# Eight batches of windowed attention and a two-layer MoE block: the casts to bf16 issued head by head, and part of set-up's loads moved behind the last pair's weights

## The chip, the cores and the metric

The kernel runs on one core of a Trainium2 chip. The metric is the device time in microseconds, the median of several executions. The core's engines are called here by the profile's names: PE (TensorE), DVE (VectorE), ACT (ScalarE), POOL (GpSimd) and SP (the sync engine, which here only issues DMAs).

## The reference, cut to what matters

q, k and v are [8 batches, 8 heads, 576 tokens, 64], f32. Eight token indices are global.

```
scores = q k^T / sqrt(64)
mask = (|i - j| <= 32) or i is global or j is global
attn = softmax(scores where mask, else -1e9)
x = (attn v), heads side by side: [4608 tokens, 512]
h = x @ w_in                      # w_in [512, 2048]
g = h + sin(alpha * h)^2 / (alpha + 1e-9)
out = g @ w_out                   # w_out [2048, 512]
```

Everything comes in as f32; the kernel multiplies in bf16.

## The kernel before, in words

The batches are handled one after the other. For batch b there is attention over four pairs of heads (`attention`), then the first product with the snake function in 16 groups of 128 columns (`gemm1`, a group being eight matmuls of 288 columns on PE, sin and square on ACT or DVE, and the sum on DVE, L1150, into H2). The second product (`gemm2`) is a generator of single matmuls; `fill(n)` takes n of them. Those of batch b are strewn into the attention of batch b+1 and the products that follow, so that PE has work while ACT and DVE make the weights. The whole order is written out by hand: what stands in the Python text first stands first in its engine's queue, and each engine works through its own queue in order.

**Weights of attention.** For each pair hp, `scores` puts keys against queries in two halves g on PE, ACT takes the exponential into the tile E (L822), and DVE multiplies by the mask (`cover`, L831). `denominators` sums the weights, `numerators` multiplies by the values, and `normalise` writes the tile xT that `gemm1` reads (L908). In batch 0 the masks are applied after `beside(hp)`.

**Casts.** From batch 2 on, q, k and v of a batch are cast to bf16 by POOL's DMAs from DRAM to DRAM (qd, kd, vd). SP then loads them: `turn_q` and `turn_k` by DMA transpose, `load_v` plainly, `load_vg` for the global tokens' values. qd and vd are one DMA each (`cast_heads`, L334, 576 KB), kd is eight, one a head (`cast_k`, L339, 72 KB). `pace(src)` (L348) is a copy of one element by POOL into the tile `seen`: POOL waits in it until src is written, and all that it issues later waits with it. In `gemm1` of batches 1 to 5 one such copy, on the first group's result, stands ahead of all three casts of batch b+2, at the second group (`CASTS`). The casts of k and v of batch 2 stand in batch 0's `gemm1` at group 13, with no pace of their own.

**Set-up.** q and k of batches 0 and 1 are loaded "lying" (`load_lying`, L452) and turned on PE. v of batch 0 comes in twelve DMAs (`load_v0`, L387), with half of w_in (columns 0 to 1023) among them, in two loads of 512 KB (L422). SP meanwhile gathers the global rows of v. VGb, their cast on POOL (L594), waits for these gathers. Behind it POOL issues the lying loads of batch 1 with the second half of w_in (1024 KB), v of batch 1 (vd) and both halves of w_out (L428). alphaT is turned on PE at L671 and copied by ACT at L681; its reciprocal recipT is made on DVE in `set_recip`, called from `beside` after pair 1 of batch 0.

Of the kernel before, what the change touches and what calls it, by code (L numbers as in the profile page):

```python
# [16 lines left out]
P = 128  # L17
# [232 lines left out]
def kernel(  # L250
# [84 lines left out]

    def cast_k(b):
        cast[b, "kd"] = dramp.tile([KT, NT12, H, D], DT.bfloat16, name="kd")
        for h in range(H):
            nc.gpsimd.dma_start(  # L339
                out=cast[b, "kd"][:, :, h], in_=k[b, h].rearrange("(i a) d -> a i d", a=KT)  # L340
            )

# [41 lines left out]
    def load_v0():  # L384
        for half in range(2):
            for m in range(NT6):
                nc.gpsimd.dma_start(  # L387
                    out=VX[0][half * D : half * D + KT, m + half],
                    in_=v[0].rearrange("h (n m a) d -> n m a h d", n=2, a=KT)[half, m],
                )  # L390
            load_w_in((0,), slice(half * CT // 2, (half + 1) * CT // 2))

# [25 lines left out]

    def load_w_in(gs, cs=slice(0, CT)):
        for g in gs:  # L420
            cols = slice(g * DFF // 2, (g + 1) * DFF // 2)
            nc.gpsimd.dma_start(  # L422
                out=w_in[:, cs, cols], in_=moe_w_in[:, cols].rearrange("(c p) n -> p c n", p=P)[:, cs]
            )
# [167 lines left out]
    gather(v, gv)  # L592
    load_v0()
    nc.gpsimd.tensor_copy(out=VGb[:], in_=gv.rearrange("p h d -> p (h d)"))  # L594
    for hps in (early, late):
        for w in (1, 0):
            load_lying(1, w, hps)
        if hps == early:
            load_w_in((1,))
    gather_heads(k, gk)  # L600
# [69 lines left out]
    turn_lying(0, 0, banks_of[0])  # L670
    nc.tensor.transpose(out=both[:, 0:NT], in_=arow[:], identity=idf[0:NT, 0:NT])  # L671
    pg = [both[:, 32 + w * 32 : 64 + w * 32] for w in range(2)]
# [7 lines left out]
    place_lying(0, 1, 0, banks_of[0][1], act)  # L680
    act(out=alphaT[:], in_=both[:, 0:NT])  # L681
    place_lying(0, 0, 0, banks_of[0][0], dve)
# [27 lines left out]

    def set_recip():
        nc.vector.tensor_scalar(out=recipT[:], in0=alphaT[:], scalar1=1e-9, scalar2=None, op0=ALU.add)
        nc.vector.reciprocal(out=recipT[:], in_=recipT[:])
# [68 lines left out]
    def attention(b, beside):  # L782
# [136 lines left out]
        def first_batch():  # L919

            for hp in range(NHP):
                Es[hp] = pairp.tile([P, 2, NT6, WCOL], DT.bfloat16, name="E")
                for g in range(2):
                    scores(hp, g)
                    if hp == 0:
                        cover(hp, g)
                if hp == last:
                    for half in (1, 0):
                        edge_tile(half)
                    nc.gpsimd.tensor_copy(out=seen[0:1], in_=VX[0][0:1, NT6, 0, 0:1])  # L930
                    cast_v(1)
                    load_w_out((0, 1))
                beside(hp)
                for g in range(2 * (hp > 0)):
                    cover(hp, g)
                if hp:
                    denominators(hp - 1)
            release_ring()
            for hp in range(2):
                inverse(hp)  # L940
                first_numerators(hp)
            inverse(last - 1)
# [17 lines left out]
        for hp in range(NHP):  # L960
            Es[hp] = pairp.tile([P, 2, NT6, WCOL], DT.bfloat16, name="E")
            scores(hp, 0)
# [109 lines left out]
    TURNED, PLACED, GLOBALS = (4, 7, 10, 13), (5, 8, 11, 14), 12  # L1072
    CASTS, TURNS = 1, 1


    def gemm1(b):
# [23 lines left out]
        for nt in range(NT):  # L1100
# [5 lines left out]
            if b == 0 and nt == 1:  # L1106
# [152 lines left out]

    waiting, copied, at_group = [], [None], [None]  # L1260

# [15 lines left out]
    def phase_a(b_att, b_moe):  # L1277
        def beside(at):

            if b_att == 0:  # L1280
                copy = nc.vector.tensor_copy
                if at in (0, 2):
# [89 lines left out]
```

## Time and profile before

| | us |
|---|---|
| median of 3 runs | 343.97 |
| lowest and highest run | 343.32, 344.09 |
| the profiled execution, its time | 344.07 |
| the profiled execution, its span | 342.3 |
| PE busy in it | 314.9 |
| ACT, DVE, POOL busy | 278.5, 252.4, 94.4 |

The profile is one execution. A row of the timeline has the start and the length in us, the engine, the line, the operation, the tiles written and read, the shapes and the count; in brackets stand the engine's idle time just before and what ended it. "issue" there means that the engine waited for nothing that the profile shows. A DMA row has the size and the time from issue to landing. In the DMA view q0 is the queue of POOL's DMAs (software), q1 that of SP's (hardware) and q8 fetches instructions; the shares of a queue are of 16 engines' time, and overlapping packets can add up to more than 100%.

### The profile page before, as it was taken

How to read it: one execution, taken by the hardware profiler on the slowest of the kernel's cores; microseconds unless marked ns; L12 is line 12 of the kernel's file. 1: busy time of each engine (PE TensorE's matmuls, PEld its weight loads, DVE VectorE, ACT ScalarE, POOL GpSimd, SP SyncE). 2: the span in 40 equal slices, each digit the busy share in tenths (PEclk: the TensorE clock that was granted, in tenths of full speed). 3: DMA queues.
4: the chain of work that ended last, by engine and by line, in shares of the span. 5: the costliest groups of instructions: out<-in, count | busy, mean ns of one | idle time of the engine just before them, and what ended most of it. 6: DMA issues, size and time to landing. Idle time of an engine off the chain costs nothing.

```text
span 342.3 us, 11579 instructions
## 1 busy us (share of the span) xinstructions
PE 314.9 (92%) x4812; PEld 202.0 (59%) x4812; DVE 252.4 (74%) x484; ACT 278.5 (81%) x406; POOL 94.4 (28%) x132
## 2 busy tenths in 40 slices
PE   0758989899989999999999999999989999999994
PEld 0646764467546765566556765676556755665543
DVE  4856896677875888777876778678757888788930
ACT  6757988788989889988899889888888888889621
POOL 7955342325300830062203520073000000003600
PEclk9999999999999999999999999999999999999999
DMA  7999999989991999199937996199929111010232
GB/s 106 125 155 201 187 225 172 168 171 161 163 131 50 165 174 169 66 148 164 166 93 139 160 153 119 46 171 176 158 57 163 33 33 69 1 33 0 78 93 67
DMA packets 140195, 41.98 MB, mean 123 GB/s; under 512 B 125194, under 2 KB 134538, under 8 KB 140138
## 3 DMA queue, kind: packets, MB, share of 16 engines
q0 software_dynamic: 98352, 18.50, 68.6%
q1 hardware_dynamic: 41786, 22.69, 34.3%
q8 instruction: 38, 0.62, 0.8%
q14 instruction: 19, 0.16, 0.1%
HBM read 41.95 MB, written 20.77 MB: 183 GB/s over the span
## 4 chain that ended last, share of the span: by engine, by line
PE 73%; DMA 9%; SPq 5%; ACT 4%; issue 4%; DVE 3%; POOL 0%; DVEq 0%; ACTq 0%; POOLq 0%
PE zo L1202 34%; PE zn L1094 11%; PE zd L1094 9%; PE zr L1094 9%; DMA w_out<-in_moe_w_out_dram 8%; PE ring L814 3%; PE zd L862 2%; PE zn L862 2%; DVE H L1150 2%; SPq L514 2%; SPq L508 1%; ACT sb L1144 1%; ACT L980 1%; SPq L504 1%; DMA SQ<-in_q_dram 1%
## 5 line engine op out<-in xcount | busy, mean ns | idle before, releaser
L1202 PE MATMUL zo<-w_out,H 128*128 128x512 bf16 (+1 forms) x576 | 147.1, 377 | 0.9 <-DMA w_out<-in_moe_w_out_dram 0.6
L1094 PEld LDWEIGHTS <-w_in 128*128 128x128 bf16 x1024 | 99.6, 98 | 45.1 <-issue 9.9
L1202 PEld LDWEIGHTS <-H 128*128 128x128 bf16 x592 | 53.7, 98 | 46.7 <-issue 1.0
L1094 PE MATMUL zn<-xT,w_in 128*128 128x288 bf16 (+1 forms) x384 | 57.0, 287 | 3.2 <-DVE H L1150 3.2
L1094 PE MATMUL zr<-xT,w_in 128*128 128x288 bf16 x320 | 47.7, 287 | 0.3
L1150 DVE SCALAR_TENSOR_TENSOR H<-s,recipT,zn 128x576 bf16<-128x576 bf16 (+1 forms) x48 | 39.5, 822 | 11.4 <-ACT s L1147 7.0
L1094 PE MATMUL zd<-xT,w_in 128*128 128x288 bf16 x320 | 46.3, 288 | 0.3 <-DVE H L1150 0.2
L822 ACT ACTIVATE E<-ring 128x720 bf16<-128x720 f32 x46 | 35.8, 778 | 13.2 <-PE ring L814 12.5
L1144 ACT ACTIVATE sb<-zn,alphaT 128x576 bf16<-128x576 f32 (+1 forms) x48 | 35.6, 742 | 11.6 <-PE zn L1094 11.1
L339 POOL DMA_DIRECT2D kd<-in_k_dram x48 | 34.6, 1162 | 34.7 <-DMA qd<-in_q_dram 30.9
L1149 DVE TENSOR_TENSOR s<-sb 128x576 bf16<-128x576 bf16 (+1 forms) x70 | 32.6, 466 | 12.4 <-ACT sb L1144 12.2
L1147 ACT ACTIVATE s<-sb 128x576 bf16<-128x576 bf16 (+1 forms) x58 | 40.0, 689 | 1.8
L831 DVE TENSOR_TENSOR E<-E,MASKT 128x720 bf16<-128x720 bf16 x64 | 33.4, 528 | 9.8 <-ACT E L822 7.8
L1150 DVE SCALAR_TENSOR_TENSOR H<-s,recipT,zd 128x576 bf16<-128x576 bf16 (+1 forms) x40 | 32.9, 822 | 7.5 <-ACT s L1147 5.0
L1150 DVE SCALAR_TENSOR_TENSOR H<-s,recipT,zr 128x576 bf16<-128x576 bf16 (+1 forms) x40 | 32.9, 822 | 6.2 <-ACT s L1147 4.6
L1144 ACT ACTIVATE sb<-zd,alphaT 128x576 bf16<-128x576 f32 (+1 forms) x40 | 29.6, 739 | 5.2 <-PE zd L1094 5.1
L1144 ACT ACTIVATE sb<-zr,alphaT 128x576 bf16<-128x576 f32 (+1 forms) x40 | 29.6, 740 | 4.3 <-PE zr L1094 4.3
L1209 ACT COPY osb<-zo 128x512 f32<-128x512 f32 (+1 forms) x36 | 20.9, 580 | 10.9 <-PE zo L1202 7.2
L814 PEld LDWEIGHTS <-KX 64*64 64x64 bf16 x896 | 15.7, 112 | 21.6 <-issue 21.0
L1192 POOL COPY H<-H 128x11 bf16 (+1 forms) x16 | 7.2, 448 | 76.7 <-DVE H L1150 75.9
L348 POOL COPY seen<-H 1x1 bf16<-1x1 bf16 x5 | 0.9, 178 | 94.3 <-DVE H L1150 94.3
L779 ACT ACTIVATE R<-L,shift 128x576 f32<-128x576 f32 x32 | 24.8, 779 | 0.6 <-DVE xT L908 0.2
(165 smaller groups left out, 351.3 us busy)
## 6 DMA issues: line engine op xcount, KB each, us to landing
VF<-vd SPq DMA_DIRECT2D x14, 336.0 KB
vd<-in_v_dram POOLq DMA_DIRECT2D x7, 576.0 KB, 10.4
qd<-in_q_dram POOLq DMA_DIRECT2D x6, 576.0 KB, 12.6
kd<-in_k_dram POOLq DMA_DIRECT2D x48, 72.0 KB, 10.8
w_out<-in_moe_w_out_dram POOLq DMA_DIRECT2D x2, 1024.0 KB, 24.4
out_dram<-osb SPq DMA_DIRECT2D x7, 256.0 KB
out_dram<-osb SPq DMA_DIRECT2D x8, 224.0 KB
out_dram<-osb SPq DMA_DIRECT2D x8, 192.0 KB
```

Of the source, the lines that this page charges most:

```text
L339: nc.gpsimd.dma_start(out=cast[b, "kd"][:, :, h], in_=k[b, h].rearrange("(i a) d -> a i d", a=KT))
L779: nc.scalar.activation(out=R[:], in_=L[:], func=AF.Exp, scale=-1.0, bias=shift[:, 0:1])
L814: nc.tensor.matmul(out=z[half * D : (half + 1) * D, t, 0 : G3 * WCOL].rearrange("p (m x c) -> p m x c", x=2, c=60)[:, m % G3, :, c0:c1], l ...
L822: nc.scalar.activation(out=weights(hp, g), in_=z[:, :, 0 : G3 * WCOL], func=AF.Exp, scale=scale)
L831: nc.vector.tensor_tensor(out=Eg, in0=Eg, in1=MASKT[:, None, G3 * g : G3 * (g + 1), :].rearrange("p o m c -> p o (m c)").to_broadcast([P, ...
L1094: nc.tensor.matmul(out=h_part, lhsT=w_in[:, c, nt * P : (nt + 1) * P], rhs=xT[:, c, lo:hi], start=(c == 0), stop=(c == CT - 1), skip_group ...
L1144: nc.scalar.activation(out=sb[:, 0:W], in_=h, func=AF.Sin, scale=alphaT[:, nt : nt + 1])
L1147: nc.scalar.activation(out=s2[:, 0:W], in_=sb[:, 0:W], func=AF.Square)
L1149: nc.vector.tensor_tensor(out=s2[:, 0:W], in0=sb[:, 0:W], in1=sb[:, 0:W], op=ALU.mult)
L1150: nc.vector.scalar_tensor_tensor(out=H2[:, nt, r0 : r0 + W], in0=s2[:, 0:W], scalar=recipT[:, nt : nt + 1], in1=h, op0=ALU.mult, op1=ALU.add,)
L1202: nc.tensor.matmul(out=ops[:, cols], lhsT=H2[:, nt, blk * P : (blk + 1) * P], rhs=w_out[:, nt, cols], start=(nt == 0), stop=(nt == NT - 1) ...
L1209: nc.scalar.copy(out=osb[:, cols], in_=ops[:, cols])
```

## The change

There are three edits.

1. `cast_one` takes the place of `cast_k`, and from batch 2's v and k on each cast is one head (72 KB). In `gemm1` of batches 1 to 5, every group from the second on may begin with a pace copy on the group before and one or two heads: q and k of batch b+2, one head a group and the sixteenth with the fifteenth; in batch 1's `gemm1` two a group, v of batch 2 first. v of batch b+1 is cast during the attention of batch b (from b = 2): three heads beside pair 2, paced on the placed queries, three beside pair 3, paced on the pair's weights, two at the end, paced on pair 2's part of xT. k of batch 2 is cast beside the four pairs of batch 1's attention, two heads each, paced on the pair's weights. q of batch 2 stays one DMA where it was. In batch 1's `gemm1`, `load_v(2)` and `load_vg(2)` move from group 2 to group 7.
2. In set-up w_in is cut into a quarter behind v's loads, a quarter, and a half. The second quarter, the lying loads of batch 1 and the half are now issued in `first_batch`, beside pair 3, behind a pace copy on that pair's weights.
3. alphaT's turn, its copy (now on DVE) and recipT are made in `set_recip`, which is called behind the numerators of pair 1.

```diff
+    def cast_one(b, name, h):
+        src = {"qd": q, "kd": k, "vd": v}[name][b, h]
...
+            nc.gpsimd.dma_start(out=dst[:, :, h], in_=src.rearrange("(i a) d -> a i d", a=KT))
+        else:
+            nc.gpsimd.dma_start(out=dst[:, h], in_=src)
...
-            load_w_in((0,), slice(half * CT // 2, (half + 1) * CT // 2))
...
     load_v0()
+    load_w_in(0, 1)
     nc.gpsimd.tensor_copy(out=VGb[:], in_=gv.rearrange("p h d -> p (h d)"))
-    for hps in (early, late):
-        for w in (1, 0):
-            load_lying(1, w, hps)
-        if hps == early:
-            load_w_in((1,))
...
-    nc.tensor.transpose(out=both[:, 0:NT], in_=arow[:], identity=idf[0:NT, 0:NT])
...
-    act(out=alphaT[:], in_=both[:, 0:NT])
...
     def set_recip():
+        nc.tensor.transpose(out=zo[0][:, 0:NT], in_=arow[:], identity=idf[0:NT, 0:NT])
+        nc.vector.tensor_copy(out=alphaT[:], in_=zo[0][:, 0:NT])
...
                 if hp == last:
+                    pace(Es[hp][0:1, 0, 0, 0:1])
+                    load_w_in(1, 2)
+                    for hps in (early, late):
+                        for w in (1, 0):
+                            load_lying(1, w, hps)
+                        if hps == early:
+                            load_w_in(2, 4)
...
                 first_numerators(hp)
+            set_recip()
             inverse(last - 1)
...
-    CASTS, TURNS = 1, 1
+    TURNS, LATE = 1, 7
+    cast_at = {}
+    for bm in range(1, B - 2):
+        pieces = [(bm + 2, name, h) for name in ("qd", "kd") for h in range(H)]
+        pieces = [(2, "vd", h) for h in range(H)] * (bm == 1) + pieces
...
-            if 0 < b and b + 2 < B and nt == CASTS:
-                pace(H2[0:1, 0, r0 : r0 + 1])
-                cast_heads(b + 2, q, "qd")
-                cast_k(b + 2)
-                cast_v(b + 2)
+            if 0 < nt and cast_at.get((b, nt)):
+                pace(H2[0:1, nt - 1, r0 : r0 + 1])
+                for piece in cast_at[b, nt]:
+                    cast_one(*piece)
...
-            if 0 < b and b + 1 < B and nt == TURNS + 1:
+            if 0 < b and b + 1 < B and nt == (LATE if b == 1 else TURNS + 1):
...
-                cast_k(2)
-                cast_v(2)
...
-                if at == 1:
-                    set_recip()
...
+            if (b_att, at) in cast_beside:
+                if at == NHP:
+                    pace(xTs[b_att][0:1, 2, 0:1])
+                elif at == 2 and b_att > 1:
+                    pace(QX[(b_att + 1) % 2][0:1, 0, 1, PAD + 4 : PAD + 5])
+                else:
+                    pace(newest[0][0:1, 0, 0, 0:1])
+                for piece in cast_beside[b_att, at]:
+                    cast_one(*piece)
```

POOL's queue in set-up, before (VF0 is batch 0's v, H2 holds the lying loads, VGb the global values, vd the cast v of batch 1):

```order
L387 DMA VF_91<-in_v_dram 48x8x64 x6
L422 DMA w_in<-in_moe_w_in_dram 128x2x1024
L387 DMA VF_91<-in_v_dram 48x8x64 x6
L422 DMA w_in<-in_moe_w_in_dram 128x2x1024
L594 CAST VGb<-SQ 64x512
L452 DMA H_97<-in_k_dram 48x4x768
L452 DMA H_97<-in_q_dram 48x4x768
L422 DMA w_in<-in_moe_w_in_dram 128x4x1024
```

The same place now (E is the last pair's weights):

```order
L392 DMA VF_91<-in_v_dram 48x8x64 x12
L426 DMA w_in<-in_moe_w_in_dram 128x4x512
L599 CAST VGb<-SQ 64x512
L353 COPY seen<-E 1x1
L426 DMA w_in<-in_moe_w_in_dram 128x4x512
L456 DMA H_97<-in_k_dram 48x4x768
L456 DMA H_97<-in_q_dram 48x4x768
L426 DMA w_in<-in_moe_w_in_dram 128x4x1024
```

One of the two loads of 512 KB that stood ahead of VGb stands behind it now, and behind the new copy.

POOL's queue from the end of batch 0's products into batch 1's, before (KX and QX are batch 1's turned keys and queries, qd, kd and vd the casts; the first two casts are batch 2's, the last one batch 3's):

```order
L369 COPY KX_94<-kTg 128x4x12x8
L372 COPY QX_96<-qTg 128x4x7x4 x2
L339 DMA kd<-in_k_dram 576x1x64 x8
L334 DMA vd<-in_v_dram 4608x1x64
L348 COPY seen<-H_97 1x1
L334 DMA qd<-in_q_dram 4608x1x64
```

And in a later batch now, from the attention of batch 2 into its products (QX is batch 3's queries, E pair 3's weights, xT the attention's result, H the first group's result; vd is batch 3's, qd batch 4's):

```order
L353 COPY seen<-QX_96 1x1
L346 DMA vd<-in_v_dram 576x64 x3
L353 COPY seen<-E 1x1
L346 DMA vd<-in_v_dram 576x64 x3
L353 COPY seen<-xT 1x1
L346 DMA vd<-in_v_dram 576x64 x2
L353 COPY seen<-H_97 1x1
L346 DMA qd<-in_q_dram 576x64
```

Where POOL issued a whole cast behind one copy, it now issues one to three heads behind each.

More of the change, by code (lines that the diff above doesn't have):

```diff
@@ L334, in cast_heads @@
         nc.gpsimd.dma_start(out=cast[b, name][:], in_=src[b].rearrange("h s d -> s h d"))
[L336 to L341, printed above, removed]
+    def cast_one(b, name, h):
+        src = {"qd": q, "kd": k, "vd": v}[name][b, h]
+        tiles = name == "kd"
+        if h == 0:
+            cast[b, name] = dramp.tile([KT, NT12, H, D] if tiles else [S, H, D], DT.bfloat16, name=name)
+        dst = cast[b, name]
+        if tiles:
+            nc.gpsimd.dma_start(out=dst[:, :, h], in_=src.rearrange("(i a) d -> a i d", a=KT))
+        else:
+            nc.gpsimd.dma_start(out=dst[:, h], in_=src)
     def cast_v(b):
@@ L417, in values, with load_w_in @@
         return VX[b % 2][rows, i - half * (NT6 - 1), h, :]
-    def load_w_in(gs, cs=slice(0, CT)):
-        for g in gs:
-            cols = slice(g * DFF // 2, (g + 1) * DFF // 2)
+    def load_w_in(lo, hi):
+        if lo < hi:
+            cols = slice(lo * DFF // 4, hi * DFF // 4)
             nc.gpsimd.dma_start(
-                out=w_in[:, cs, cols], in_=moe_w_in[:, cols].rearrange("(c p) n -> p c n", p=P)[:, cs]
+                out=w_in[:, :, cols], in_=moe_w_in[:, cols].rearrange("(c p) n -> p c n", p=P)
             )
@@ L960, in attention @@
         for hp in range(NHP):
-            Es[hp] = pairp.tile([P, 2, NT6, WCOL], DT.bfloat16, name="E")
+            newest[0] = Es[hp] = pairp.tile([P, 2, NT6, WCOL], DT.bfloat16, name="E")
             scores(hp, 0)
@@ L1072 @@
     TURNED, PLACED, GLOBALS = (4, 7, 10, 13), (5, 8, 11, 14), 12
-    CASTS, TURNS = 1, 1
+    TURNS, LATE = 1, 7
[3 more added lines that the diff above has]
+        pieces = [(2, "vd", h) for h in range(H)] * (bm == 1) + pieces
+        each = 1 + (bm == 1)
+        for nt in range(1, NT):
+            cast_at[bm, nt] = pieces[(nt - 1) * each : nt * each if nt < NT - 1 else None]
+    cast_beside = {(1, hp): [(2, "kd", 2 * hp + h) for h in range(2)] for hp in range(NHP)}
+    for ba in range(2, B - 1):
+        for at, hs in ((2, range(3)), (3, range(3, 6)), (NHP, range(6, H))):
+            cast_beside[ba, at] = [(ba + 1, "vd", h) for h in hs]
     def gemm1(b):
@@ L1257, in gemm2_globals @@
         )
-    waiting, copied, at_group = [], [None], [None]
+    waiting, copied, at_group, newest = [], [None], [None], [None]
     def fill(n):
```

## The prediction

> **What bounds the kernel now.** I read the page first, then busy time by stage, then TensorE's idle gaps in the timeline, then GpSimd's timeline and the landings of its DMAs. The page's first rows show TensorE nearly full:
>
> ```profile
> PE 314.9 (92%) x4812; PEld 202.0 (59%) x4812; DVE 252.4 (74%) x484; ACT 278.5 (81%) x406; POOL 94.4 (28%) x132
> q8 instruction: 38, 0.62, 0.8%
> ```
>
> So only idle TensorE time can be won. The windows view, cut where the first group of products of each batch starts, shows where it is (columns: window, length, then busy time of PE, PEld, DVE, ACT, POOL, clock, DMA share, GB/s):
>
> ```profile
> 0.00:28.81 28.81, 14.68 (x569) 12.27 (x570) 18.00 (x63) 19.48 (x30) 22.81 (x45) 1.00 1.09 136
> 28.81:69.46 40.65, 36.48 (x740) 23.70 (x739) 30.74 (x54) 33.39 (x51) 13.81 (x17) 1.00 1.66 191
> 69.46:106.89 37.43, 35.83 (x529) 22.66 (x528) 28.75 (x53) 33.10 (x50) 9.94 (x11) 1.00 1.32 141
> ...
> 180.41:216.70 36.29, 36.29 (x535) 23.17 (x533) 28.18 (x52) 32.46 (x49) 9.92 (x11) 1.00 1.24 135
> 216.70:254.86 38.16, 36.71 (x535) 23.23 (x533) 28.18 (x52) 32.94 (x50) 9.92 (x11) 1.00 1.26 133
> 254.86:291.06 36.20, 36.20 (x533) 23.11 (x533) 29.07 (x51) 30.96 (x46) 0.00 (x0) 1.00 0.34 73
> ```
>
> The clock is full throughout. The window without casts (254.86 on: GpSimd 0.00, DMA share 0.34) takes 36.20 us with no TensorE idle time. The five with casts (69.46 to 254.86, 185.40 us) are 185.40 - 5 x 36.20 = 4.40 us longer together, but not alike: 1.23 the first, 0.09 the fourth, 1.96 the last. The gaps themselves, from TensorE's timeline (start, length, in brackets the idle time before and what ended it):
>
> ```profile
> 21.28 0.23 PE L814 MATMUL ring<-QX,KX 64*64 64x32 bf16 x1 [2.41 <-issue]
> 22.68 0.58 PE L708 MATMUL zo<-VGb,pick 64*128 64x512 bf16 x1 [0.85 <-POOL VGb L594]
> 56.20 2.10 PE L1202 MATMUL zo<-w_out,H 128*128 128x512 bf16 x9 [0.60 <-DMA w_out<-in_moe_w_out_dram]
> 68.02 0.21 PE L862 MATMUL zn<-E,VF 56*64 56x32 bf16 x4 [1.24 <-issue]
> 99.64 0.41 PE L862 MATMUL zd<-E,ones 56*64 56x120 bf16 x20 [0.87 <-issue]
> 249.10 0.49 PE L862 MATMUL zn<-E,VF 56*64 56x88 bf16 x27 [0.94 <-issue]
> ```
>
> The "issue" gaps fall in the middle of a run of like matmuls (the first alone follows as the last one of its fourteen, x1), all in stages of many short matmuls, and no semaphore ends them. TensorE lacked instructions. Those come by DMA: q8 above, 38 packets of 16 KB, and one of them lies just ahead of the gap at 99.64, while the software queue is full with the cast of v:
>
> ```profile
> q0 software_dynamic: 1695, 0.22, 127.9%
> q8 instruction: 1, 0.02, 2.3%
> ```
>
> That is the DMA view of 97.0 to 99.7 us. So I read the gaps as instruction fetches that share DMA engines with the casts. Against it stands the window from 180.41: casts like the others' and no gap.
>
> **The change part by part: set-up.** GpSimd's rows and the landing times (last number of a DMA row, from issue):
>
> ```profile
> 12.78 0.77 POOL L422 DMA_DIRECT2D w_in<-in_moe_w_in_dram  x1
> 17.22 0.79 POOL L422 DMA_DIRECT2D w_in<-in_moe_w_in_dram  x1
> 22.03 0.60 POOL L594 CAST VGb<-SQ 64x512 bf16<-64x512 f32 x1 [4.02 <-DMA SQ<-in_k_dram]
> 23.19 0.58 POOL L452 DMA_DIRECT2D H<-in_q_dram  x1
> 23.76 0.77 POOL L422 DMA_DIRECT2D w_in<-in_moe_w_in_dram  x1
> w_in<-in_moe_w_in_dram POOLq DMA_DIRECT2D x1, 1024.0 KB, 12.0
> H<-in_q_dram POOLq DMA_DIRECT2D x1, 288.0 KB, 6.8
> 21.55 0.77 ACT L822 ACTIVATE E<-ring 128x720 bf16<-128x720 f32 x1 [2.69 <-PE ring L814]
> 24.02 0.98 DVE L831 TENSOR_TENSOR E<-E,MASKT 128x720 bf16<-128x720 bf16 x2
> 14.61 0.21 DVE L712 TENSOR_SCALAR recipT<-alphaT 128x16 f32<-128x16 f32 x1
> 14.86 0.25 DVE L713 RECIPROCAL recipT<-recipT 128x16 f32<-128x16 f32 x1
> 28.43 27.72 DMA w_out<-in_moe_w_out_dram
> ```
>
> Before, two loads of 512 KB of w_in leave at 12.78 and 17.22. After, one leaves behind all twelve loads of v, at about 17.22 - 0.77 = 16.5; the second 512 KB waits for VGb's cast and the last pair's weights (call that moment T). The gathers that VGb waits for then share the DMA engines with 512 KB less. GpSimd has been idle for 4.02 us when VGb starts at 22.03, so it can come at 18.0 at the earliest, and no later than now unless the new load hinders the last gather. I take 19.5 to 20. With the 2.41 us gap halved, the weights (21.55 + 0.77) come about 1.2 earlier, so T is about 21 or a little before. TensorE then reaches the products up to 3.26 us earlier (2.41 + 0.85), at least 0; I take 1.8.
>
> What gives it back is w_out: its second half lands at 28.43 + 27.72 = 56.15, and TensorE was waiting already (0.60). The software queue's loads land in the order of issue: the last 1024 KB of w_in land at 23.76 + 12.0 = 35.8 and the load ahead of it at 23.19 + 6.8 = 30.0, so 512 KB cost 2.9 us. That much is moved behind T. But the queue was not full there (22 to 24, 24 to 26 and 26 to 28 us):
>
> ```profile
> q0 software_dynamic: 147, 0.27, 73.5%
> q0 software_dynamic: 100, 0.15, 75.9%
> q0 software_dynamic: 270, 0.39, 107.3%
> ```
>
> It lacked 0.12 + 0.24 MB of the 0.39 per 2 us, 1.8 us of transfer. So w_out lands 2.9 - 1.8 = 1.1 us later if T stays at 22.6, and about 0.6 us earlier if T comes 1.7 earlier. Whatever else TensorE wins in set-up it waits for here. Ends for set-up: -2.2 to +2.9; I take -0.6, the end nearer to the row with the wait. The loads that the products need have room: w_in's second half landed at 35.8 and its use begins eight groups of 1.2 us (below) after 28.81, at 38.4; the first 512 KB are wanted at 28.81.
>
> The pace copy on the last pair's weights stands before DVE's masking of the same tile (24.02 above), so DVE waits for GpSimd; at T of 21 to 22.8 that is hidden, and costs T - 24 if VGb slips past 24. Alpha's transpose, copy and the reciprocal move behind the numerators of pair 1: three DVE instructions of about 0.21, 0.21 and 0.25 us (the copy taken like L712) that stood off the path at 14.6 stand just before its sums of pair 2. DVE waits for ScalarE at places there, so I take +0.15, ends 0 and 0.67.
>
> **Batch 1's attention (28.81:69.46).** kd and vd of batch 2 no longer start behind w_out in one lump; kd goes two heads per pair, vd into the next products. The gap of 1.24 lay under that lump. I take -1.0, ends -1.24 and 0. turn_q(2) needs qd, which still follows w_out; its queries are placed at the very end of that attention, so 1 us late is covered.
>
> **Batches 2 to 6.** Per batch, one pace copy and three large groups of DMAs become 24 heads with 17 or 18 pace copies:
>
> ```profile
> 74.15 0.18 POOL L348 COPY seen<-H 1x1 bf16<-1x1 bf16 x1 [11.29 <-DVE H L1150]
> 74.82 2.20 POOL L334 DMA_DIRECT2D qd<-in_q_dram  x1 [0.49 <-issue]
> 87.72 0.64 POOL L339 DMA_DIRECT2D kd<-in_k_dram  x1 [6.00 <-DMA qd<-in_q_dram]
> kd<-in_k_dram POOLq DMA_DIRECT2D x48, 72.0 KB, 10.8
> qd<-in_q_dram POOLq DMA_DIRECT2D x6, 576.0 KB, 12.6
> 75.43 0.98 PE zr L1094 x8
> 76.63 0.98 PE zd L1094 x8
> ```
>
> GpSimd: 24 x 0.64 + 18 x 0.18 = 18.6 us against 9.9, of a 36 us period: hidden, as only casts queue behind its waits; its other late work, the columns' loads and copies of the last batch, comes after. The last two rows (chain of waits) put groups of products 1.20 us apart. One head per group takes 0.82 us, so pacing holds; with batch 1's two per group (1.46 us) GpSimd falls behind and those casts run as a stream until 74.2 + 12 x 1.46 = 91.7. Heads don't cost more transfer: kd went head by head before and landed in 10.8, whole qd in 12.6. On the sync queue the order is unchanged; load_v now waits for the last two heads of v, issued after pair 2's result, while pair 3 is still to be multiplied; it stands in the third group and its values are used a whole product stage later. Zero, at worst 0.5. The gain is the stalls: 0.87 + 0.94 seen, 4.40 at most by the periods. I take -1.6, ends 0 and -4.4: in attention six heads of v now fall in its second half, so not all go.
>
> Sum: -0.6 + 0.15 - 1.0 - 1.6 = -3.05 us on the profiled execution's 344.07 (span 342.3 and 1.8 around it; the median of the runs is 343.97, 0.1 less): 341.0.
>
> **The rivals.** *Stalls indifferent to the casts* (0.19): the window from 180.41 has casts and no gap. Then each gap returns at another place and only set-up and DVE count: 344.07 - 0.6 + 0.15, about 343.6, or 343.4 to 344.4. Here the Trainium skill speaks against the change ("DMA: Bandwidth & Descriptors", Queues, rings and completion order): each DMA engine goes round its queues packet by packet, so a fetch waits for a packet of each, however long the casts' backlog is; by that rule this rival is the case. The gap at 99.64 under a full queue speaks against it, the one at 249.10 for it: there the software queue was at 41.9%:
>
> ```profile
> q0 software_dynamic: 660, 0.08, 41.9%
> ```
>
> (246.0 to 249.1 us.) *w_out late* (0.13, slower): VGb does not come earlier, T stays at 22.6 or later, and the moved 512 KB delay w_out by 1.1 (queue as idle as before) to 2.9 us, straight into the wait at 56.20. With batches 2 to 6 unchanged this is 345.2 to 347.0, say 346.0. It decides from T of about 21.5 on: 22.6 less 1.1. *All idle goes* (0.08): 4.40, 1.24 and 0.6: 344.07 - 6.24 + 0.15 = 338.0.
>
> **How the numbers follow.** The forecast has 0.60, its own range 339.2 to 343.2 (half to one and a half times its gain). The range of 338.6 to 344.9 holds it, the indifferent stalls and the shallow end of the late w_out; outside stay most of the slower rival and of the largest gain, under 0.2. A measurement here tells 0.2%, 0.69 us, from no change. Faster by more: 0.60 + 0.08 + 0.06 of the indifferent case = 0.74; within: 0.12; slower: 0.14.
>
> **What would show it.** Right: the gap at 21.28 under 1.3 us, VGb's cast before 21, w_out's wait under 1 us, no issue gap over 0.5 us in batches 1 to 6 and periods of 36.2 to 36.6; GpSimd's waits for qd (6.00 above) gone. Wrong: TensorE waiting over 1.5 us for w_out, w_in or the lying loads; DVE waiting for GpSimd's pace copy; TensorE gaps of the same sum in other batches; the sync queue held at load_v so that stores are late.

## The result and the profile after

The changed kernel took 340.3 us (median of 8 runs, 339.32 to 341.94), the kernel before, run beside it, 344.03 (8 runs, 342.86 to 346.06). The ratio is 0.9891, with an interval of 0.9864 to 0.9919: faster, as forecast (341.0), by 0.7 us more. The profiled execution took 340.73 with a span of 339.0.

The windows of the changed kernel, cut where each batch's first product starts (columns as before):

```profile
0.00:28.41 28.41, 15.81 (x569) 12.57 (x570) 20.03 (x64) 20.51 (x29) 24.18 (x46) 1.00 1.09 137
28.41:68.15 39.74, 37.14 (x734) 24.12 (x738) 29.95 (x54) 32.42 (x50) 11.79 (x18) 1.00 1.50 188
68.15:104.69 36.54, 34.84 (x522) 22.71 (x529) 28.63 (x53) 33.04 (x50) 20.89 (x44) 1.00 1.41 144
104.69:141.63 36.94, 35.54 (x526) 23.17 (x533) 28.98 (x56) 32.90 (x50) 19.06 (x44) 1.00 1.19 134
141.63:177.89 36.26, 35.31 (x526) 23.19 (x533) 28.49 (x55) 32.20 (x49) 19.15 (x42) 1.00 1.32 139
177.89:214.30 36.41, 35.56 (x526) 23.22 (x533) 28.30 (x52) 32.53 (x49) 17.47 (x39) 1.00 1.27 136
214.30:251.73 37.43, 35.79 (x527) 23.23 (x534) 28.20 (x52) 32.89 (x50) 20.36 (x47) 1.00 1.38 135
251.73:287.90 36.17, 35.22 (x526) 23.09 (x533) 29.09 (x51) 31.00 (x46) 1.39 (x3) 1.00 0.49 84
```

Read the lengths only: this trace lacks records of some matmuls (x526 for PE where PEld has x533), so PE's busy time can't be set against before's. Set-up is 28.81 - 28.41 = 0.40 us shorter, the window of batch 1's attention 40.65 - 39.74 = 0.91, and the five with casts take 251.73 - 68.15 = 183.58 in place of 185.40, so 1.82 less. That makes 3.1 of the 3.3 us by which the span shrank. The last window before, 36.20, is 36.17 now. Each of these is one execution. How far one can be trusted is seen from the kernels below with the same set-up: their first products start between 28.04 and 28.95, so the 0.40 of set-up is not clear of that spread. Six more kernels with the casts as changed take 182.90 to 183.39 for the five windows, all well under 185.40.

TensorE's timeline at the places shown for before, and at the first products of batch 0:

```profile
19.08 0.51 PE L814 MATMUL zn<-QX,KX 64*64 64x120 bf16 x14 [0.51 <-issue]
19.52 0.61 PE L706 MATMUL zo<-VGb,pick 64*128 64x512 bf16 x1
23.93 0.51 PE L862 MATMUL zd<-E,ones 56*64 56x120 bf16 x16 [0.74 <-issue]
26.59 0.79 PE L862 MATMUL zd<-E,VF 56*64 56x88 bf16 x28 [0.75 <-DVE GD L756]
28.41 1.64 PE L1113 MATMUL zn<-xT,w_in 128*128 128x288 bf16 x6
29.85 1.64 PE L1113 MATMUL zr<-xT,w_in 128*128 128x288 bf16 x6
245.98 0.49 PE L862 MATMUL zn<-E,VF 56*64 56x88 bf16 x26 [0.24 <-issue]
```

From batch 1's attention on only one issue gap over 0.2 us is left, 0.24; w_out's wait and the gaps of 1.24, 0.87 and 0.94 are gone. In set-up the gap of 2.41 is 0.51 and the values' product (L706) comes 22.68 - 19.52 = 3.16 us earlier. Most of this is lost again before the products: a new issue gap (0.74), a new wait for DVE (0.75), and matmuls at half pace. Six products of 288 columns take 1.64 us, where before they took 0.90; the clock column says 1.00 all the same. GpSimd's timeline and, last row, DVE's:

```profile
18.09 0.80 POOL L599 CAST VGb<-SQ 64x512 bf16<-64x512 f32 x1 [0.77 <-DMA SQ<-in_k_dram]
19.47 0.18 POOL L353 COPY seen<-E 1x1 bf16<-1x1 bf16 x1 [0.58 <-ACT E L822]
19.70 0.76 POOL L426 DMA_DIRECT2D w_in<-in_moe_w_in_dram  x1
23.60 2.16 POOL L334 DMA_DIRECT2D vd<-in_v_dram  x1
24.05 2.12 DVE L712 TENSOR_SCALAR recipT<-alphaT 128x16 f32<-128x16 f32 x1
```

VGb's cast is there 3.9 us earlier and T is 19.5. The last row is the surprise: the 128x16 addition of the reciprocal, 0.21 us before, takes 2.12 where it now stands, and TensorE waits behind it (the 0.75 above). The median landing times on the page:

```profile
kd<-in_k_dram POOLq DMA_DIRECT2D x48, 72.0 KB, 4.6
vd<-in_v_dram POOLq DMA_DIRECT2D x48, 72.0 KB, 3.8
qd<-in_q_dram POOLq DMA_DIRECT2D x40, 72.0 KB, 6.3
```

k landed in 10.8 before and whole q in 12.6: a head no longer waits behind a batch's whole casts.

### The profile page after: what moved, and what is told of

It reads as the page before. It is cut to its first block, busy times and chain, and to the rows that moved or that the text cites. A ratio compares the mean times of both kernels' runs of the same rounds, so it can differ in the third digit from the quotient of the medians.

```text
span 339.0 us, 11821 instructions
## 1 busy us (share of the span) xinstructions
PE 310.8 (92%) x4753; PEld 202.9 (60%) x4812; DVE 253.9 (75%) x485; ACT 278.5 (82%) x405; POOL 142.5 (42%) x296
## 4 chain that ended last, share of the span: by engine, by line
PE 77%; DVE 7%; ACT 6%; issue 4%; DMA 3%; POOL 2%; DVEq 0%; POOLq 0%; ACTq 0%
PE zo L1218 32%; PE zn L1113 13%; PE zr L1113 10%; PE zd L1113 9%; PE ring L814 4%; DVE H L1166 3%; PE zd L862 3%; ACT sb L1160 2%; PE zn L862 2%; DVE s L1165 1%; DMA H<-in_q_dram 1%; DMA out_dram<-osb 1%; ACT L988 1%; ACT s L1163 1%; ACT L L772 1%
## 5 line engine op out<-in xcount | busy, mean ns | idle before, releaser
L1218 PE MATMUL zo<-w_out,H 128*128 128x512 bf16 (+1 forms) x517 | 134.3, 377 | 6.1 <-issue 5.1
L1113 PE MATMUL zn<-xT,w_in 128*128 128x288 bf16 (+1 forms) x384 | 58.0, 291 | 3.5 <-DVE H L1166 2.8
L1113 PE MATMUL zr<-xT,w_in 128*128 128x288 bf16 x320 | 48.5, 291 | 0.3
L344 POOL DMA_DIRECT2D kd<-in_k_dram x48 | 31.2, 653 | 9.1 <-issue 7.3
L346 POOL DMA_DIRECT2D vd<-in_v_dram x48 | 30.4, 643 | 1.8 <-issue 1.3
L346 POOL DMA_DIRECT2D qd<-in_q_dram x40 | 25.3, 633 | 8.2 <-issue 5.1
```

The costliest lines, as they stand in the source:

```text
L344: nc.gpsimd.dma_start(out=dst[:, :, h], in_=src.rearrange("(i a) d -> a i d", a=KT))
L346: nc.gpsimd.dma_start(out=dst[:, h], in_=src)
L1113: nc.tensor.matmul(out=h_part, lhsT=w_in[:, c, nt * P : (nt + 1) * P], rhs=xT[:, c, lo:hi], start=(c == 0), stop=(c == CT - 1), skip_group ...
L1218: nc.tensor.matmul(out=ops[:, cols], lhsT=H2[:, nt, blk * P : (blk + 1) * P], rhs=w_out[:, nt, cols], start=(nt == 0), stop=(nt == NT - 1) ...
```

## The experiments

**Theory.** TensorE's instructions come in blocks by DMA; a block whose fetch falls into a dense stretch of casts comes late, and TensorE stands. Spreading the casts takes them off the fetches. **Rivals**: the gaps belong to places in the program; smaller DMAs help, not their spreading; the gain is set-up's.

### Which edit gives what

*Casts alone, set-up alone, and everything but the moved reciprocal.* In the second k and v of batch 2 are cast where they were before; in the third alpha's turn and copy are back too:

```diff
 # casts only: edits 2 and 3 undone
+    for hps in (early, late):            # behind VGb's cast, as before
+        for w in (1, 0):
+            load_lying(1, w, hps)
...
 # set-up only: edit 1 undone
+            if 0 < b and b + 2 < B and nt == 1:
+                pace(H2[0:1, 0, r0 : r0 + 1])
+                cast_heads(b + 2, q, "qd")
+                cast_k(b + 2)
+                cast_v(b + 2)
...
 # all but edit 3
-            set_recip()                  # behind pair 1's numerators
...
+                if at == 1:
+                    set_recip()
```

> The kernel before with edit 1 alone: casts head by head, set-up and recipT as before. Forecast's theory (lumps of casts delay TensorE's instruction fetches, and w_out's load is not touched by them): the issue gaps of 1.24, 0.87 and 0.94 us go, set-up keeps its 2.41, 0.85 and 0.60; the sum of the windows of batches 2 to 6 falls from 185.4 to about 183.6; 341 to 342. Rival (fetch gaps are indifferent to casts, the gain is all set-up's): 343.5 to 344.3 and gaps of the same sum.

> The kernel before with edits 2 and 3 alone: whole casts as before. Forecast's theory: no gain in batches 2 to 6 (185 us for the five windows), set-up as in the changed kernel (VGb's cast near 18, the second quarter of w_in near 19.7), and the start of batch 1's products within 1 us of before's 69.46; 343 to 344.5. Rival (the gain is set-up's): 340 to 341.5.

> The changed kernel with edit 3 undone: alphaT turned and copied in set-up and recipT made beside pair 1, as before the change. In the changed kernel's profile the instruction that makes recipT took 2.12 us on DVE instead of 0.21, TensorE then waited 0.75 us, and its matmuls ran at 0.24 us apart instead of 0.12 until 31.9. Theory A (the late recipT stands behind GpSimd's issue of a whole cast, and the pause costs TensorE its clock): the wait and the slow matmuls go, products of batch 0 start at about 26 to 27 instead of 28.41 and the third group at about 31 instead of 34.20; w_out's landing takes back part; 338 to 339.5, against 340.3. Rival B (the slow matmuls come from the earlier start alone, or w_out takes all back): 340 to 341.

Measured: casts alone 341.6 us, ratio to before 0.9897 (0.9863 to 0.9931); set-up alone 343.49, 0.9955 (0.9926 to 0.9984); all but edit 3 340.54, 0.9871 (0.9832 to 0.991); the whole change, as above, 0.9891. So the casts bring nearly all of it. The two parts come to 1.03% and 0.45%, the whole to 1.09%; the intervals are too wide to say whether they add up. With casts alone no issue gap stands in batches 1 to 6 and the five windows take 183.33; with set-up alone they take 184.94 and gaps are back at the old places, the one of batch 2 only as 0.29 at 99.47 (TensorE's timeline of the set-up-only kernel):

```profile
68.42 0.21 PE L869 MATMUL zn<-E,VF 56*64 56x32 bf16 x3 [1.23 <-issue]
249.04 0.49 PE L869 MATMUL zn<-E,VF 56*64 56x88 bf16 x26 [1.30 <-issue]
```

Without edit 3 the addition takes 0.17 us, batch 1's attention starts at 52.05 in place of 53.45, and then w_out takes all of it back (TensorE's timeline of that kernel):

```profile
50.44 0.82 PE L1217 MATMUL zo<-w_out,H 128*128 128x512 bf16 x3 [0.52 <-DMA w_out<-in_moe_w_out_dram]
57.22 1.02 PE L1217 MATMUL zo<-w_out,H 128*128 128x512 bf16 x4 [1.83 <-DMA w_out<-in_moe_w_out_dram]
```

Its first product of batch 1 comes at 68.56, that of the whole change at 68.15, and its time is rival B's. In these kernels what set-up wins ends at w_out, and w_out itself does not come at a fixed time: its second half landed at 57.18 here, at 55.73 in the changed kernel and at 56.16 before. Theory A was right that the wait of 0.75 and the slow matmuls go, but batch 0's products start at 27.97, not at 26 to 27.

### Is it the fetches?

*Casts that nobody reads, put into the window without casts.* First early, at the second group of batch 6's products, then so late that they meet the fetches of batch 7's attention:

```diff
+            if b == B - 2 and nt == 1:        # the second kernel: nt == 13
+                pace(H2[0:1, nt - 1, r0 : r0 + 1])
+                cast_heads(B - 1, q, "qx")
+                for h in range(H):
+                    cast[B - 1, "kx", h] = dramp.tile([S, D], DT.bfloat16, name="kx")
+                    nc.gpsimd.dma_start(out=cast[B - 1, "kx", h][:], in_=k[B - 1, h])
+                cast_heads(B - 1, v, "vx")
```

> The changed kernel with one more lump, for nothing: in batch 6's products, the stage without casts, whole casts of q, k and v of batch 7 into scratch tensors, paced on the first group as the kernel before paced them. The output is unchanged. Forecast's theory (a lump delays fetches): gaps marked issue appear in batch 7's attention, the window from the start of batch 6's products to that of batch 7's grows from 36.17 by 0.5 to 2 us, the time by as much. Rival (indifferent): 36.2 to 36.4 and the time as the changed kernel's, 340.3.

> The changed kernel with one more thing: in the products of batch 6 at group 13, behind a pace copy on group 12 (about 268 us), whole casts of q, k and v of batch 7 to DRAM that nobody reads. In the changed kernel the stretch from the first product of batch 6 to that of batch 7 (251.7 to 287.9) has no casts, takes 36.17 us and has no TensorE gap; two or three instruction fetches fall between 268 and 290. Fetch theory (a fetch is slowed by packets of casts that are under way, and a late fetch stops TensorE): the fetches that start between about 270 and 288 come late against the instructions, an issue gap of 0.3 to 1.5 us appears in the attention of batch 7, and that stretch takes 36.5 to 37.7. Rival (the gaps were set by the program's places, and casts only happened to be there): no gap, 36.1 to 36.3. What comes after 287.9 may be longer for another reason, since the last batch's row loads queue behind the added casts; that part is not read.

The early lump changed nothing: window 36.17, no gap, 340.84 us (ratio 0.9892, 0.984 to 0.9944). My expectation missed that it had drained by about 275, before the next fetch. The late one hit: 342.49 us (0.9955, 0.9929 to 0.998). Its window, TensorE's timeline, and the DMA view from 276 to 278, just ahead of the fetch:

```profile
250.46:288.64 38.18, 36.37 (x533) 23.21 (x533) 29.33 (x51) 31.11 (x46) 9.93 (x14) 1.00 1.07 127
281.59 0.20 PE L862 MATMUL zd<-E,ones 56*64 56x32 bf16 x1 [1.81 <-issue]
q0 software_dynamic: 2219, 0.34, 236.6%
```

A window that takes 36.17 without casts takes 38.18, more than the 36.5 to 37.7 that I had expected, and an issue gap stands in a place that never had one. So the gaps come with the casts and aren't set by the program alone.

The DMA records give the start of each 16 KB instruction packet, and the records of TensorE's instructions how far it is by then. Packets are numbered from 0. A block is taken as 256 instructions of TensorE: a matmul and its weight load count two, and each of the 26 or 27 others on record (mostly waits on semaphores) counts one. The count in the table is what TensorE has begun when packet n starts, less 256 n. It can pass 256, since packet n need not bring block n.

```
kernel                      packet  start    count  TensorE stands
before                         8     65.46    396    66.78-68.02
before                        11     97.15    398    98.77-99.64
before                        28    246.66    412   248.16-249.10
changed                     8/11/28    -   301/306/323    -
no casts from batch 3 (below) 11/28    -     179/226      -
set-up only                   28    246.61    415   247.73-249.04
casts nobody reads, late      32    279.19    385   279.78-281.59
changed                       32    276.95    259      -
heads in a row (below)        15    137.49    447   138.24-140.07
whole but spread (below)      11     98.08    449    97.15-100.61
```

In all the kernels together 17 issue gaps over 0.3 us stand from batch 1's attention on. In each TensorE had stopped at a count of 449 or 450, whichever packet it was, and each gap ended 2.3 to 2.7 us after that packet's start (the packets themselves took 0.9 to 1.3). So I read it that TensorE stops where its fetched instructions end, and goes on some time after the packet is in. Why the number is 449 or 450 the records don't say. What casts shift is the packet's start: packet 11 starts at a count of 179 without casts, at 306 with heads spread out and at 398 with whole casts. What holds it up ahead of its start, the records don't show. The Trainium skill ("Runtime: NRT & Kernel Launch", Instruction fetch mechanics) has the refill in blocks of 256 instructions, which agrees with stops that lie whole blocks of 256 apart; it calls the cost mostly hidden, and in these runs it wasn't.

*Split without spreading, and spread without splitting.*

```diff
 # heads in a row, at the old places
+            if 0 < b and b + 2 < B and nt == 1:
+                pace(H2[0:1, 0, r0 : r0 + 1])
+                cast_q(b + 2)             # eight cast_one each
+                cast_k(b + 2)
+                for h in range(H):
+                    cast_one(b + 2, "vd", h)
...
 # whole, at about the new places
+            cast_at[bm, 1], cast_at[bm, 9] = [(bm + 2, "qd", None)], pieces[8:]
...
+        cast_beside[ba, 2] = [(ba + 1, "vd", None)]
```

> The changed kernel with its casts back at the old places (q, k and v of batch b+2 behind one pace copy at the second group of products; k and v of batch 2 at group 13 of batch 0's products), but all of them still one head a DMA, 24 in a row. It differs from the kernel with whole casts and the new set-up (343.5, five stretches 184.9 together) only in that q and v go by heads, and from the changed kernel (340.3; 183.6) only in when the heads are issued. Theory 1, spreading is what helps: issue gaps are back in batches 1, 2 and 6, five stretches of 184.4 to 185.4, time 343.0 to 344.0. Theory 2, splitting is what helps (a DMA of 576 KB holds the rings, one of 72 KB doesn't): gaps stay away, 183.3 to 183.9, time 340.0 to 340.9.

> The changed kernel with q's and v's casts whole again (one DMA of 576 KB), but each at about its new place: q of batch b+2 at the second group of products, k's eight heads at the tenth, v of the next batch beside pair 2; in batch 1 v at the second, q at the sixth, k at the eleventh group. Against heads at the old places (347.1) it is the other half of the edit: spread, not split. Theory 1, what counts is that not all casts of a batch are under way at once: few gaps, five stretches 183.2 to 184.2, time 340.0 to 341.2. Theory 2, each lump of 576 KB is enough to make the fetch that falls into it late: gaps of 0.5 to 1.5 us in most attentions, stretches 184.5 to 186, time 342 to 344.

Heads in a row: 347.09 us, slower than before (1.0077, 1.0042 to 1.0111), five windows of 188.20 together. Set against whole casts at the same places (set-up alone, 184.94), splitting by itself does harm. Whole but spread: 344.47, not told from before (0.998, 0.9944 to 1.0016). One row of each kernel's timeline of TensorE, the worst gap:

```profile
140.07 0.34 PE L822 MATMUL ring<-QX,KX 64*64 64x120 bf16 x11 [1.83 <-issue]
```

```profile
100.61 0.61 PE L865 MATMUL zd<-E,ones 56*64 56x120 bf16 x19 [3.46 <-issue]
```

The second kernel had only two such gaps, but one lump that meets a fetch is enough. Neither half of the edit works alone; both theories that I had set against each other there were too simple.

*What casts still cost.* The casts of batches 3 to 7 are left out and batch 2's are read in their place.

```diff
     def cast_one(b, name, h):
+        if b > 2:
+            cast[b, name] = cast[2, name]
+            return
```

> The changed kernel without the casts of batches 3 to 7: their q, k and v are those of batch 2, so the output is another one; the pace copies stay. It gives the price that casts have left. If casts cost TensorE time only by late fetches and those were already in time after the change, the five stretches take what they take now, 183.6, and the time is 340 to 340.6. If every microsecond over the quiet stretch is the casts', they take 5 x 36.2 = 181.0, with the first one perhaps still longer, since batch 2's casts are still under way: time 337.5 to 338.3. If casts are not to blame for the first and the fifth stretch (36.5 and 37.4 after the change) these stay as they are, and only 0.3 to 0.8 goes: 339.5 to 340.1.

339.77 us (0.9875, 0.9839 to 0.9911). Its windows of batches 1 to 6:

```profile
67.33:103.55 36.22, 35.73 (x528) 22.69 (x528) 28.57 (x53) 32.73 (x50) 8.04 (x23) 1.00 0.77 111
103.55:140.50 36.95, 36.46 (x535) 23.12 (x534) 28.84 (x56) 32.93 (x50) 3.98 (x18) 1.00 0.40 87
140.50:176.71 36.21, 36.21 (x533) 23.15 (x533) 28.55 (x55) 32.22 (x49) 4.48 (x19) 1.00 0.53 92
176.71:212.97 36.26, 36.26 (x535) 23.16 (x533) 28.19 (x52) 32.44 (x49) 3.82 (x17) 1.00 0.45 86
212.97:249.96 36.99, 36.52 (x534) 23.11 (x533) 28.21 (x52) 32.94 (x50) 4.40 (x20) 1.00 0.44 89
```

The second and the fifth stay at 37.0: their excess has nothing to do with casts (0.45 of it is a wait of the fourth group of products for DVE). The floor of the five is 182.63, not 5 x 36.2 (v of batch 2 is still cast in the first of them). So the casts cost 185.40 - 182.63 = 2.77 us before, and after the change 0.95 in its profiled execution; the six other kernels with the changed casts, at 182.90 to 183.39, leave 0.3 to 0.8.

### Set-up

*The reciprocal last.* `set_recip()` stands behind the last pair's `normalise`, where GpSimd has issued that cast.

```diff
-            set_recip()               # behind pair 1's numerators
...
             normalise(last)
+            set_recip()
```

> The changed kernel with alphaT's turn, copy and the reciprocal behind the last pair's placed products of batch 0 instead of behind pair 1's numerators. There GpSimd is no longer issuing the cast of v of batch 1 (2.16 us, at 23.6). Theory 1, DVE's 128x16 addition took 2.12 us because of GpSimd's issue beside it: it takes 0.17 to 0.25 us, the wait of 0.75 us at 26.6 goes, the first products of batch 0 start at about 27.6 instead of 28.4. Theory 2, the instruction is slow at this place by its own input (a copy just before, cold code): it takes about 2 us there too, and the first sine waits for it. Under theory 1 w_out, which lands at about 55.7, is what the kernel then waits for: a wait of 0.5 to 1.5 us for w_out in batch 1's attention, and the time stays at 339.9 to 340.7. If w_out were no limit the time would be 339.3 to 339.7.

339.87 us (0.9874, 0.984 to 0.9909). DVE's timeline, then TensorE's:

```profile
28.12 0.18 DVE L712 TENSOR_SCALAR recipT<-alphaT 128x16 f32<-128x16 f32 x1
56.28 1.46 PE L1218 MATMUL zo<-w_out,H 128*128 128x512 bf16 x6 [0.62 <-DMA w_out<-in_moe_w_out_dram]
```

Theory 1 holds: 0.18 us. In each of the seven kernels that have the addition under GpSimd's issue of whole vd it ended 0.41 to 0.42 us after that issue did, and took 1.57 to 2.28 (in the changed kernel it ended at 26.17, the issue at 25.76): it was held until then. Not every issue holds it: beside that of w_out (0.89 us from 28.01, in a kernel below) it took 0.17. Nor does the cast's issue hold every instruction: the copy of alphaT out of PSUM took 0.16 at 23.85, inside it. In another kernel below (q by heads alone) the addition met GpSimd's own cast of the global keys and queries (0.63 us from 29.18), took 0.56 and ended 0.04 us behind it. The Trainium skill states such a lock ("SBUF — State Buffer", Who interferes with whom): VectorE's `tensor_scalar` in a two-port mode and GpSimd block each other for a whole instruction. The trace agrees for the issue of the casting DMA and for GpSimd's own cast, and shows no block for w_out's issue. The products start at 27.80, 0.6 earlier, and w_out's wait (0.62) is there at once. The time can't be told from the changed kernel's.

*v of batch 1 held back from w_out, and q of batch 2 by heads.* Three kernels on top of the last one: the first edit, both, the second.

```diff
 # v later
+            if b == 0 and nt == 13:
+                nc.sync.dma_start(out=later[:], in_=H2[0:1, 11, r0 : r0 + 1])
+                load_v(1)
+                load_vg(1)
...
 # q of batch 2 by heads
-                cast_heads(2, q, "qd")
+    cast_beside = {(1, hp): [(2, "qd", 4 * hp + h) for h in range(4)] for hp in range(2)}
...
-            if b_moe == 0 and at == 0:
+            if b_moe == 0 and at == 2:
                 turn_q(2)
```

> The kernel with the reciprocal last (339.9), and the loads of v and of the global values of batch 1 held on the sync queue behind a tiny store of group 11 of batch 0's products, so that they no longer share the DMA engines with the first half of w_out from 41.7 us on. Theory 1, what set-up wins is given back at w_out, which competes with those loads: w_out's halves land 1.5 to 3 us earlier (about 45 to 46 and 53 to 54), the wait of 0.62 us for it at 55.7 goes, the first product of batch 1 comes 0.6 us earlier (67.1 instead of 67.7), time 339.0 to 339.6. Rival, v takes the place of w_out as the late one: its loads then share with w_out's second half, the products of batch 1's first pair (about 56) wait for VF, and the time is 339.9 to 341.

> The kernel with the reciprocal last and the loads of v of batch 1 held back (341.7 in its own session, profiled at 340.75), and q of batch 2 no longer cast whole behind w_out, but four heads beside pair 0 and four beside pair 1 of batch 1's attention; k of batch 2 follows beside pairs 2, 3 and the end, and the turning of q of batch 2 is asked for two pairs later. There the fetch that started at 58.59 fell into the whole cast of q (the software queue moved 260 to 290 KB in every 2 us from 56 to 60) and TensorE stood 1.30 us until 61.03. Fetch theory: with the heads spread that gap goes, w_out's wait stays away too, and the first product of batch 1 comes at 66.6 to 67.0 instead of 68.08; span about 337.7, time 338.6 to 339.5, below both kernels. Rival, the later heads are late: queries of batch 2 are placed later, and the attention of batch 2 or the next turning of k waits 0.5 us or more, or the fetch meets the heads instead and the gap stays at over 0.8: time 339.8 to 341.

> The same spreading of q of batch 2 without holding back v's loads: the kernel with the reciprocal last (339.9, first product of batch 1 at 67.69) plus that edit. There no fetch was late in batch 1's attention, and the wait for w_out was 0.62. If w_out is then the only thing that holds batch 1, nothing changes: first product of batch 1 at 67.5 to 67.9, time 339.6 to 340.2. If the whole cast of q took DMA time from w_out's second half, w_out lands earlier than 56.24 and the wait shrinks.

v later alone: 341.73 us (0.9897, 0.9863 to 0.9932). w_out's second half lands at 54.34 and its wait is gone, but the next row of TensorE's timeline comes in its place, at a place where the whole cast of q of batch 2 now meets a fetch:

```profile
61.03 0.20 PE L862 MATMUL zd<-E,ones 56*64 56x32 bf16 x2 [1.30 <-issue]
```

My rival named v as the late one; it was the fetch. With q by heads too that gap is gone and batch 1's products start at 66.53, as expected, 1.6 us ahead of the changed kernel. Then it is lost at the queries of batch 2 (DVE's timeline, then TensorE's):

```profile
72.53 0.83 DVE L366 COPY QX<-qt 128x1152 bf16<-128x1152 bf16 x2 [4.46 <-DMA qt<-qd]
74.69 1.02 PE L1115 MATMUL zn<-xT,w_in 128*128 128x288 bf16 x7 [3.98 <-DVE H L1170]
```

DVE places these queries at the end of batch 1's attention, their turning is asked for at 64.44, and all of DVE's queue waits. A fetch is late there too (0.94 at 102.02). 345.62 us, 1.0041 (0.9999 to 1.0082). q by heads without the first edit has the same wait (3.54); its six runs lie between 341.53 and 347.4, with a ratio of 0.9957 (0.9893 to 1.0022), which says nothing either way. Its w_out landed no earlier (57.14), so nothing shows that the whole cast of q held it. No version here beats the changed kernel by more than the intervals.

## Why the prediction was right, step by step

- **What bounds it: idle TensorE time, stalls of instruction fetch that go with the casts.** Shown, by the lump at the fetch and by 17 gaps with one and the same stop. The rival by which fetches don't care for the casts falls: there a fetch that started at a count of 259 started at 385 under casts. TensorE had passed 259 at 275.50 and the packet started at 279.19, so 3.7 us later (0.2 in the changed kernel), while the casts' packets in the 3 us ahead of it took 0.03 us at the median and 0.74 at most; a turn of one packet for each queue, on which this rival rested in part, doesn't come to that. Two things had spoken for it. The window from 180.41 before (casts and no gap) fits the table: its fetches started at counts up to 228, far from 449. And the 41.9% at the gap of 249.10 was read in the wrong stretch, most of it behind the packet's start at 246.66. In the DMA view of 244 to 246, ahead of it, the casts' queue is full:

```profile
q0 software_dynamic: 2221, 0.28, 222.1%
```

- **Batches 2 to 6, -1.6: measured -1.82**, and in five kernels that keep both the heads and their spreading and have no added casts there (the changed one, casts only, without edit 3, early lump, reciprocal last) the gaps stay away. The upper end, 4.40, was wrong: it took the quiet window for the floor of all; 1.6 of it was other work. 2.77 was to be had. For the same reason the periods of 36.2 to 36.6, given as a sign of being right, held in three windows only; the others take 36.94 and 37.43, and 36.95 and 36.99 without casts.
- **Batch 1's attention, -1.0: measured -0.91**, but as a sum of other things. From its first scores to the next products it is 2.50 us shorter (53.45 to 68.15 against 52.26 to 69.46): the gap of 1.24, w_out's 0.60 and a smaller issue gap of 0.30 are gone; the other 0.36 I have not traced. The products ahead of it are 1.59 longer, since they begin at half pace (the fourth group starts 5.79 us after the first in place of 4.13).
- **Set-up, -0.6: measured -0.40 at the first product**, which is no more than these starts differ among themselves, and the way there was misread. T came at 19.5, not 21, and TensorE was 3.16 us ahead at L706. I had w_out take the surplus; it would have (the kernel without edit 3 shows 0.52 + 1.83), but the new issue gap, the reciprocal and the slow matmuls took it first, so that w_out, landing at 55.73, met no wait. That these gains and losses came out near -0.6 was luck.
- **The reciprocal, +0.15 with ends 0 and 0.67: the step that failed.** I summed three DVE instructions at the durations they had at 14.6, where GpSimd did something else beside them. At the new place one took 2.12 and TensorE waited 0.75. It cost nothing measurable in the end: with the wait gone (reciprocal last, and without edit 3) w_out's wait stood in its place.
- **GpSimd's load**: 18.6 us a period forecast, 17.47 to 20.89 measured, hidden. Its waits for whole q (6.00) are gone; heads wait for heads 1.13 and 0.52 us once each in batch 1, where the casts stream as forecast, and once 2.82 us in batch 5's products (at 228.06).
- *w_out late* was to decide from T of 21.5 on, and that was too late a bound. In the ten kernels with this set-up and with v of batch 1 loaded where it was, T lay between 19.07 and 20.44, and w_out's second half landed at 55.40 to 57.18, in six of them behind before's 56.16. By the prediction's sum (56.15 + 1.1, less what T gains on 22.6) the landings should have been 1.6 to 3.1 us earlier than they were; which of its terms is short isn't traced. In the changed kernel, at 55.73, no harm came of it.
- *The range.* 339.2 to 343.2 is not half to one and a half times the gain of 3.05, as the text says; that would be 339.5 to 342.5. The result lies in both.

What stays open: what holds a fetch up ahead of its packet (a full queue doesn't always do it: packet 24 before started at a count of 185, 0.7 us behind a stretch of casts at over 240%); why the first products of batch 0 run at half pace in some kernels (14 matmuls in the changed one, 8 with the casts alone, 10 with the reciprocal last, none before and without edit 3), which the late reciprocal can't be alone, since the casts-only kernel has it at the old place; and whether queries placed later would keep the 1.6 us of the last kernels.

## What to carry to other kernels

A stall that ends on no semaphore, in a run of short matmuls, may be a late instruction fetch, as all such stalls over 0.3 us were here: look for the instruction packet some 2.4 us ahead of its end, and at what the DMA queues carry ahead of the packet's start, not at the gap. Background DMAs were worth making both small and paced; small ones in a row, or whole ones at good places, gained nothing here. And a step that is moved doesn't take its old duration along: look at what the other engines do at the new place.

## What the hardware showed that I had not expected

- TensorE stopped at the same point, a count of 449 or 450, at all 50 issue gaps over 0.3 us of the fourteen traces, set-up's included.
- 24 casts of 72 KB in a row made a fetch later than the same bytes in one DMA for q, eight for k and one for v: packet 15 started at a count of 447 in the one kernel, 346 in the kernel before and 341 with set-up alone; packets 8 and 28 started at 395 and 417, about as with set-up alone (395 and 415).
- The gap of 2.41 at 21.28 was in part replaced by the one of 0.74 at 23.93, at the next fetch: packet 2 started at a count of 374, and of 271 before. That the moved loads did this isn't shown, since the casts-only kernel, with set-up's loads as before, has a gap of 0.78 at the same packet (count 345).
- Matmuls of 288 columns started every 0.24 us, in place of 0.12, with the granted clock shown as 1.00.
